# Reordering the two products of a mixture-of-experts half expert, and splitting softplus' eviction into deferred pieces

## The chip, the cores and the metric

One core of one Trainium2 chip runs the whole program. The metric is the device time of one execution in microseconds (us). The core's engines each work through a queue of their own, in order: TensorE (PE, matmuls and their weight loads PEld), VectorE (DVE), ScalarE (ACT), GpSimd (POOL) and SyncE (SP, which only issues DMAs here). TensorE accumulates in PSUM, in banks of 128 x 512 f32; the other operands are in SBUF.

## The reference

Three stages, all in float32: causal attention with a cumulative bias (2 batches, 8 heads, 576 tokens, head dimension 64), a mixture of 8 experts whose gates are balanced by 8 Sinkhorn steps, and a feed-forward layer with softplus. N = 1152 tokens, model width 512.

```python
def _moe_ref(x, w_gate, w1, w2):          # w1: 8 x 512 x 1024, w2: 8 x 1024 x 512
    ...                                   # P: gates, N x 8
    for e in range(E):
        h = np.maximum(x @ w1[e], 0.0)
        ye = h @ w2[e]
        out += P[:, e:e + 1] * ye

def _moe2_ref(x, w_in, w_out):            # 512 x 2048, 2048 x 512
    h = x @ w_in
    g = np.maximum(h, 0.0) + np.log1p(np.exp(-np.abs(h)))
    return (g @ w_out).astype(np.float32)
```

## The kernel before, in words

After attention, both feed-forward stages run as one loop over 20 half experts x of 512 hidden columns: 0 to 15 with Relu (two for each of 8 experts), 16 to 19 with softplus (the second layer). Every f32 operand is split into a high part in fp32r and a low part (xh and xl, w1h and w1l, w2h and w2l, hh and hl), and each product is three matmuls: high by high, high by low, low by high.

The first product, h = x @ w1, is done by Strassen's scheme. A Unit is one part p (of two) of a half expert's columns for one batch g of 576 tokens, and has seven products p1 to p7 of six matmuls with 288 columns each. Products accumulate in PSUM banks: the bank a takes p1, p6, p5, p3; the bank c takes p7 and p4; p2 has a bank of its own. Between products ScalarE copies a out to SBUF (v1 after p1, u2 after p6, u4 after p5), and since the next product adds to the same bank, TensorE waits for the copy. VectorE adds the copies to the other banks (t1 after p2, t2 after p5 and p4) and each result is evicted: for Relu hh = Relu(z) on ScalarE and hl = max(z, 0) - hh on VectorE. For softplus the eviction is Abs, Exp, Ln on ScalarE, two sums on VectorE, one on POOL, and then, in `post`, POOL's last sum, ScalarE's copy into hh and VectorE's difference hl.

The second product is written as rows: one of nine tiles of 128 tokens (`downs`), each of four quarters of three matmuls with 512 columns, after which the result is added into acc by VectorE (by ScalarE's copy in the first half of each layer). A row reads hh and hl of all four column blocks. Row 4 straddles the two batches. Rows use two PSUM banks in turn, so row t + 2 waits for the sum of row t.

The order on each engine is the order in which this Python code records instructions; no scheduler moves them. `late` holds evictions that are put off: each product ends with `flush()`, which records them all. `back` holds preparations (prep1 splits w1 of the next half, prep2 splits w2 of this one); `bg()` records one step of them. `quarter()` records a quarter of a row, a step of `bg` and, every so often, a step of the gates (in the first two halves) or of `convert`, which turns the second layer's float64 weights into f32 in pieces of 512 columns on VectorE, ScalarE and POOL and writes them to DRAM from POOL's queue. `turn` transposes acc for the second layer: batch 0 beside the last rows of half 15, batch 1 at the start of half 16.

Of a half's four Units, (p 0, batch 0) runs beside rows 5 to 8 of the half before. The next three run without rows beside them: (0, 1), (1, 0) and (1, 1) as far as p7, 18 products. The rest of the last one, p5, p3, p4, runs beside rows 0 to 3 (in halves 0 and 16 the first Unit runs without rows too, 25 products):

```python
for z in "dddPdddPdddPddddddd":            # d: a quarter, P: a product of the last Unit
...
for z in "PddPddPddPdPdddPddPdddd":        # P: a product of the next half's first Unit
```

## Time and profile before

| what | value |
|---|---|
| median of 3 runs (lowest, highest) | 1327.45 us (1326.55, 1327.57) |
| the profiled execution | 1327.69 us, span 1325.9 us |
| PE, PEld busy | 1127.5 us (85%), 975.9 us (74%) |
| DVE, ACT, POOL busy | 825.1 us (62%), 539.1 us (41%), 393.6 us (30%) |

Busy time is a share of the whole span, and the span has stages with different limits, so the stages are read apart. Attention ends near 122 us; the 16 ReLU half experts follow until 953 us, the four softplus half experts until 1321.5 us. In the profile's 40 slices of some 33 us TensorE is busy for nine tenths or more from slice 9 to slice 29, and for four to seven tenths, with one slice of nine, in the last ten; the granted clock is full in the former and 0.6 to 0.9 in the latter. An engine's idle time matters only where TensorE, or what ends the stage, waits for it.

### The profile page before, as it was taken

To read this page: it belongs to the slowest core of one execution; us is meant where nothing else is said; L and a number is where in the kernel's file an instruction comes from. 1 tells how busy PE (TensorE), PEld (TensorE's weight loads), DVE (VectorE), ACT (ScalarE), POOL (GpSimd) and SP (SyncE) were. 2 spreads that over 40 slices of the span, in tenths; PEclk is the share of its full clock that TensorE was granted. 3 is DMA by queue.
4 is the path that set the end of the run, shared out by engine and by line. 5 is a ranking of instruction groups with operands and counts; after the bars stand their busy time and mean duration, and the time that the engine had idled before them with its cause. 6 is when DMAs were issued, how large, how long until landed. Compare 5 with 4: busy or idle time off the path is not lost.

```text
span 1325.9 us, 17763 instructions
## 1 busy us (share of the span) xinstructions
PE 1127.5 (85%) x6596; PEld 975.9 (74%) x6596; DVE 825.1 (62%) x1575; ACT 539.1 (41%) x1138; POOL 393.6 (30%) x489
## 2 busy tenths in 40 slices
PE   6998998999999999999999999999954946756747
PEld 4766876888888888888888888889743745645635
DVE  4545456587877877877877876455554344545432
ACT  5977432234333333333233233233354444344431
POOL 8864000021312312322232222110124334334331
PEclk8978999999999999999999999999966978877869
DMA  5310101132312222222122221011010000000001
GB/s 161 106 42 13 48 33 44 35 110 73 118 58 96 100 75 96 83 86 96 71 96 96 80 74 62 32 65 48 17 32 0 33 32 17 20 29 16 0 2 71
DMA packets 30423, 78.47 MB, mean 59 GB/s; under 512 B 6048, under 2 KB 10656, under 8 KB 30336
## 3 DMA queue, kind: packets, MB, share of 16 engines
q1 hardware_dynamic: 27768, 68.93, 15.8%
q0 software_dynamic: 2560, 8.39, 1.7%
q8 instruction: 52, 0.85, 0.3%
q14 instruction: 35, 0.29, 0.1%
q10 hardware_dynamic: 8, 0.01, 0.0%
HBM read 66.02 MB, written 10.82 MB: 58 GB/s over the span
## 4 chain that ended last, share of the span: by engine, by line
PE 48%; DVE 22%; ACT 10%; POOL 10%; issue 8%; DMA 1%; SPq 0%; POOLq 0%; DVEq 0%; ACTq 0%
PE py L276 22%; PE ph L211 20%; POOL a L189 4%; DVE hl L171 3%; DVE acc L286 2%; DVE a L185 2%; PE sc L449 2%; POOL a L186 2%; ACT hh L190 2%; ACT a L181 1%; DVE t L233 1%; ACT hh L170 1%; ACT a L180 1%; DVE t L261 1%; PE pv L560 1%
## 5 line engine op out<-in xcount | busy, mean ns | idle before, releaser
L211 PE MATMUL ph<-xh,w1h 128*128 128x288 f32 x1120 | 351.9, 314 | 155.2 <-ACT u L219 124.2
L211 PEld LDWEIGHTS ph<-xh,w1h 128*128 128x128 f32 x1120 | 221.1, 197 | 184.0 <-ACT u L219 136.8
L211 PE MATMUL ph<-xl,w1h 128*128 128x288 f32 x1120 | 341.3, 305 | 0.0
L211 PE MATMUL ph<-xh,w1l 128*128 128x288 f32 x1120 | 340.8, 304 | 0.0
L276 PE MATMUL py<-w2h,hh 128*128 128x512 f32 x720 | 291.0, 404 | 16.0 <-DVE acc L283 13.1
L276 PE MATMUL py<-w2l,hh 128*128 128x512 f32 x720 | 289.1, 401 | 0.0
L276 PE MATMUL py<-w2h,hl 128*128 128x512 f32 x720 | 288.7, 401 | 0.0
L211 PEld LDWEIGHTS ph<-xl,w1h 128*128 128x128 f32 x1120 | 221.9, 198 | 8.2
L211 PEld LDWEIGHTS ph<-xh,w1l 128*128 128x128 f32 x1120 | 221.3, 198 | 0.0
L276 PEld LDWEIGHTS py<-w2h,hh 128*128 128x128 f32 x720 | 138.3, 192 | 41.5 <-DVE acc L283 14.5
L783 POOL TENSOR_TENSOR cm<-cm,ct 128x512 f32<-128x512 f32 x32 | 41.1, 1284 | 419.1 <-DVE ct L782 412.5
L276 PEld LDWEIGHTS py<-w2h,hl 128*128 128x128 f32 x720 | 138.2, 192 | 34.0
L276 PEld LDWEIGHTS py<-w2l,hh 128*128 128x128 f32 x720 | 138.2, 192 | 23.6
L170 ACT ACTIVATE hh<-t 128x288 fp32r<-128x288 f32 (+1 forms) x128 | 72.3, 565 | 189.3 <-DVE t L261 107.5
L171 DVE SCALAR_TENSOR_TENSOR hl<-t,hh 128x288 fp32r<-128x288 f32 (+1 forms) x128 | 84.2, 658 | 71.9 <-ACT hh L170 71.9
L186 POOL TENSOR_TENSOR a<-a,a 128x288 f32<-128x288 f32 x64 | 55.0, 860 | 210.2 <-DVE a L184 210.2
L219 ACT ACTIVATE u<-ph 128x288 f32<-128x288 f32 x160 | 64.6, 404 | 125.8 <-PE ph L211 125.8
L286 DVE SCALAR_TENSOR_TENSOR acc<-py,gate,acc 128x512 f32<-128x512 f32 x126 | 94.1, 747 | 29.0 <-PE py L276 28.0
L125 POOL TENSOR_TENSOR ws<-raw 128x256 f32<-128x256 f32 x40 | 31.7, 793 | 206.4 <-DVE w1l L136 148.3
L251 DVE TENSOR_TENSOR t<-ph,u 128x288 f32<-128x288 f32 x80 | 36.4, 455 | 78.8 <-ACT u L219 78.8
L191 DVE TENSOR_TENSOR hl<-a,hh 128x288 fp32r<-128x288 f32 x64 | 32.5, 508 | 84.8 <-ACT hh L190 84.8
L190 ACT ACTIVATE hh<-a 128x288 fp32r<-128x288 f32 x64 | 28.4, 443 | 95.3 <-POOL a L189 95.3
(176 smaller groups left out, 1590.1 us busy)
## 6 DMA issues: line engine op xcount, KB each, us to landing
...
```

The source lines that it names most:

```text
L170: nc.scalar.activation(out=hh, in_=src, func=AF.Relu)
L171: nc.vector.scalar_tensor_tensor(out=hl, in0=src, scalar=0.0, in1=f(hh), op0=ALU.max, op1=ALU.subtract)
L186: nc.gpsimd.tensor_tensor(out=a2, in0=a1, in1=a2, op=ALU.subtract)
L189: nc.gpsimd.tensor_tensor(out=a3, in0=a3, in1=a2, op=ALU.add)
L190: nc.scalar.activation(out=zh, in_=a3, func=AF.Copy)
L191: nc.vector.tensor_tensor(out=zl, in0=a3, in1=f(zh), op=ALU.subtract)
L211: nc.tensor.matmul(o, u, v, start=(start and c == 0 and n == 0), stop=(c == 1 and n == 2), skip_group_check=True)
L219: nc.scalar.activation(out=t, in_=self.a, func=AF.Copy)
L251: nc.vector.tensor_tensor(out=self.t2[:, HB:], in0=self.c, in1=u4, op=ALU.add)
L276: nc.tensor.matmul(py, u, v, start=(k == 0 and n == 0), stop=(k == NF - 1 and n == 2))
L286: nc.vector.scalar_tensor_tensor(out=a, in0=py, scalar=gate_t[0][:, t, e:e + 1], in1=a, op0=ALU.mult, op1=ALU.add)
L783: nc.gpsimd.tensor_tensor(out=m, in0=m, in1=f(t), op=ALU.add)
```

## The change

1. All four Units change places. `products(x, g)` makes a table of the 14 products of both parts, named a1 to a7 (part 0) and b1 to b7 (part 1), in the order a1 a2 a6 a7 a5 b1 b2 a3 a4 b6 b7 b5 b3 b4. Of batch 1, a1 a2 a6 a7 a5 run without rows; the other nine run beside rows 0 to 3. All 14 of the next half's batch 0 run beside rows 5 to 8. (Halves 0 and 16 first run 12 products of batch 0, then a1 a2 of batch 1 and b3 b4 of batch 0.) The counts of products and quarters are the same.
2. Deferred work carries a number of flushes to wait (`defer`), every quarter begins with a flush as well, and `drain` records all that is left. In the softplus halves a piece's VectorE and POOL sums (`sums`) come two flushes after its ScalarE operations, and the two last sums (`rest_`) five after (in the first stretch of half 16, one and two).
3. A softplus piece is 288 columns. POOL writes hh itself, ScalarE's copy goes, and VectorE makes hl in two sums, a3 - hh and then + a2.
4. p2's and p4's sums are written back into their PSUM banks, and evictions read them there; only p5's sum still goes to SBUF.
5. w2l is made in two sums of 512 columns for each half of w2, the second half's on POOL. A conversion item is recorded in four steps in place of two, at every third quarter in place of every sixth. Batch 1's transposes use the rows' banks.

```diff
         yield
-        nc.vector.tensor_tensor(out=lo, in0=t, in1=f(hi), op=ALU.subtract)
+        for c in range(2):
+            (nc.gpsimd if i else nc.vector).tensor_tensor(out=lo[:, c], in0=t[:, c], in1=f(hi[:, c]), op=ALU.subtract)
         load_next()
...
     late = []
+    def defer(k, x):
+        late.append([k, x])
     def flush():
-        for x in late:
+        now_ = [x for x in late if x[0] <= 0]
+        wait = [[k - 1, x] for k, x in late if k > 0]
+        late.clear()
+        for _, x in now_:
             x()
-        late.clear()
...
+        late[:0] = wait
+    def drain():
+        while late:
+            flush()
+    lag = [0, 1]
+    def evict(x, z, q, cols):
         hh, hl = hb[0][:, q, cols], hb[1][:, q, cols]
         if x < NX:
...
             return
...
+        def sums():
             nc.vector.tensor_scalar(a2, a1, 1.0, -1.0, ALU.add, ALU.add)
...
             nc.gpsimd.tensor_tensor(out=a2, in0=a1, in1=a2, op=ALU.subtract)
...
+            nc.gpsimd.tensor_tensor(out=hh, in0=a3, in1=a2, op=ALU.add)
+        def rest_():
+            nc.vector.tensor_tensor(out=a3, in0=a3, in1=f(hh), op=ALU.subtract)
+            nc.vector.tensor_tensor(out=hl, in0=a3, in1=a2, op=ALU.add)
+        defer(lag[0], sums)
+        defer(lag[1], rest_)
     class Unit:
...
             self.h1 = slice(g * S + HB, (g + 1) * S)
...
             flush()
-            t = m_t[0].tile([P, HB], F32, tag="t1", name="t1", bufs=1)
-            nc.vector.tensor_tensor(out=t, in0=b, in1=self.v1, op=ALU.add)
...
+            nc.vector.tensor_tensor(out=b, in0=b, in1=self.v1, op=ALU.add)
+            defer(0, lambda: evict(self.x, b, self.p, self.h0))
         def p6(self):
...
             u4 = self.copy("u4")
-            self.t2 = m_t[0].tile([P, S], F32, tag="t2", name="t2", bufs=1)
-            nc.vector.tensor_tensor(out=self.t2[:, HB:], in0=self.c, in1=u4, op=ALU.add)
+            t = m_t[0].tile([P, HB], F32, tag="t2", name="t2", bufs=2)
+            nc.vector.tensor_tensor(out=t, in0=self.c, in1=u4, op=ALU.add)
+            defer(0, lambda: evict(self.x, t, self.p + 2, self.h1))
         def p3(self):
...
             flush()
-            nc.vector.tensor_tensor(out=self.t2[:, :HB], in0=self.c, in1=self.u2, op=ALU.add)
...
+            nc.vector.tensor_tensor(out=self.c, in0=self.c, in1=self.u2, op=ALU.add)
+            defer(0, lambda: evict(self.x, self.c, self.p + 2, self.h0))
     def downs(x, tiles):
...
                 nc.vector.tensor_scalar(t, hi, 5, 2, ALU.logical_shift_left, ALU.logical_shift_right)
+                yield
                 nc.vector.scalar_tensor_tensor(out=t, in0=lo, scalar=29, in1=t,
...
                 nc.vector.tensor_scalar(t, t, 0xFF800000, None, ALU.bitwise_and)
+                yield
                 nc.vector.tensor_scalar(lo, lo, 28, 1, ALU.logical_shift_right, ALU.bitwise_and)
...
         def quarter(d):
+            flush()
             next(d, None)
...
             nstep[0] += 1
-            if x < 2:
-                if nstep[0] % 3 == 0:
+            if nstep[0] % 3 == 0:
+                if x < XE:
                     next(gates, None)
-            elif x < NX - 2 and nstep[0] % 6 == 0:
-                next(conv, None)
...
-        for x in range(NH):
...
+                elif x < NX - 2:
+                    next(conv, None)
+        ORDER = "a1 a2 a6 a7 a5 b1 b2 a3 a4 b6 b7 b5 b3 b4".split()
+        def products(x, g):
+            u = dict(a=Unit(x, 0, g), b=Unit(x, 1, g))
+            return {z: getattr(u[z[0]], "p" + z[1]) for z in ORDER}
+        def play(seq, todo, d=None):
+            for z in seq.split():
+                if z == "d":
+                    quarter(d)
+                else:
+                    todo.pop(z)()
+                    if d is None:
+                        bg()
         for x in range(NH):
...
             if x == NX:
...
             back += [prep2(x, 0), prep2(x, 1)]
+            c = {}
+            if first:
+                if x == NX:
+                    back.insert(0, turn(1, t_p))
+                c = products(x, 0)
+                for _ in range(2 if x == NX else 1):
+                    bg()
+                for z in ORDER[:-2]:
+                    c.pop(z)()
+                    bg(2 if x == NX else 1)
+                rest()
+            u = products(x, 1)
+            play("a1 a2", u)
+            if c:
+                play("b3 b4", c)
             if x == NX:
...
-                    rest()
...
+                drain()
...
+                lag[:] = [1, 4]
+            play("a6 a7 a5", u)
             rest()
...
+            drain()
+            d = downs(x, range(NB))
+            play("b1 d b2 d a3 d a4 d", u, d)
             back.append(prep1(x + 1, 0))
-            d = downs(x, range(NB))
...
-                    quarter(d)
+            play("b6 d b7 d b5 d d b3 d b4 d d d d d d d", u, d)
             rest()
+            drain()
             back.append(prep1(x + 1, 1))
             d = downs(x, range(NB, NTT))
-            for _ in range(NF):
-                quarter(d)
+            play("d d d d", {}, d)
             if x + 1 == NX:
...
                 for _ in range(4 * NF):
+                    flush()
                     next(d, None)
...
             elif x + 1 < NH:
...
-                        quarter(d)
+                u = products(x + 1, 0)
+                play("a1 d a2 d a6 d d a7 d a5 d", u, d)
+                rest()
+                play("b1 d b2 d a3 d a4 d b6 d b7 d b5 d d b3 d b4 d", u, d)
             for _ in d:
-                pass
+                flush()
             rest()
...
+        drain()
...
```
Three places in the queues, before and after. In the rows a number behind a name tells buffers apart.

VectorE in ReLU half 8, between the last row's sum and the sum after p2 (before) or a2 (after) of batch 1. L778 to L782 and L796, L797 belong to `convert`:

```order
L286 SCALAR_TENSOR_TENSOR acc<-py,gate,acc 128x512
L778 SCALAR_TENSOR_TENSOR cm<-cm,ct 128x512
L780 TENSOR_SCALAR ct<-ct 128x512
L781 TENSOR_SCALAR f_5476<-f_5476 128x512
L782 SCALAR_TENSOR_TENSOR ct<-f_5476,ct 128x512
L233 TENSOR_TENSOR t_5686<-ph,v_5674 128x288
L149 TENSOR_TENSOR w2l_5677<-raw,w2h_5676 128x1024
```

And after:

```order
L299 SCALAR_TENSOR_TENSOR acc<-py,gate,acc 128x512
L796 TENSOR_SCALAR f_5524<-f_5524 128x512
L797 SCALAR_TENSOR_TENSOR ct<-f_5524,ct 128x512
L245 TENSOR_TENSOR ph<-ph,v_5786 128x288
L150 TENSOR_TENSOR w2l_5789<-raw,w2h_5788 128x512 x2
L185 SCALAR_TENSOR_TENSOR hl<-ph,hh 128x288
```

Two of the four conversion operations have gone to an earlier quarter, p2's sum is written into its bank ph, and w2l is two operations, of the first half of w2 alone.

ScalarE in half 18, ahead of the copy u that p5 of the second part (b5) waits for. Before, the eviction of p4's t2 stands there:

```order
L180 ACTIVATE a_10612<-t_10549 128x288
L181 ACTIVATE a_10612<-a_10612 128x288
L182 ACTIVATE a_10614<-a_10612 128x288
L180 ACTIVATE a_10621<-t_10549 128x288
L181 ACTIVATE a_10621<-a_10621 128x288
L182 ACTIVATE a_10623<-a_10621 128x288
L190 ACTIVATE hh<-a_10614 128x288
L190 ACTIVATE hh<-a_10623 128x288
L219 ACTIVATE u_10636<-ph 128x288
```

After, the copy v of b1, and then the pieces b2, a3 and a4:

```order
L232 ACTIVATE v_10770<-ph 128x288
L191 ACTIVATE a_10784<-ph 128x288
L192 ACTIVATE a_10784<-a_10784 128x288
L193 ACTIVATE a_10786<-a_10784 128x288
L191 ACTIVATE a_10799<-ph 128x288
L192 ACTIVATE a_10799<-a_10799 128x288
L193 ACTIVATE a_10801<-a_10799 128x288
L191 ACTIVATE a_10823<-ph 128x288
L192 ACTIVATE a_10823<-a_10823 128x288
L193 ACTIVATE a_10825<-a_10823 128x288
L232 ACTIVATE u_10847<-ph 128x288
```

The two copies into hh (L190), which read POOL's sum, have gone; in front of u there are now three pieces of three operations where two pieces and their two copies were.

POOL in half 18 where w2 is split, before (the sums of four pieces; w2l is not POOL's):

```order
L186 TENSOR_TENSOR a_10469<-a_10468,a_10469 128x288
L189 TENSOR_TENSOR a_10461<-a_10461,a_10460 128x288
L189 TENSOR_TENSOR a_10470<-a_10470,a_10469 128x288
L186 TENSOR_TENSOR a_10515<-a_10514,a_10515 128x288
L189 TENSOR_TENSOR a_10516<-a_10516,a_10515 128x288
L186 TENSOR_TENSOR a_10576<-a_10575,a_10576 128x288
L189 TENSOR_TENSOR a_10577<-a_10577,a_10576 128x288
```

After (L150 is w2l of the second half of w2; a_10666 belongs to b4 of batch 0, a_10712 to a2 of batch 1, a_10750 to a5):

```order
L199 TENSOR_TENSOR a_10666<-a_10665,a_10666 128x288
L200 TENSOR_TENSOR hh<-a_10667,a_10666 128x288
L150 TENSOR_TENSOR w2l_10720<-raw,w2h_10719 128x512 x2
L199 TENSOR_TENSOR a_10712<-a_10711,a_10712 128x288
L200 TENSOR_TENSOR hh<-a_10713,a_10712 128x288
L199 TENSOR_TENSOR a_10750<-a_10749,a_10750 128x288
L200 TENSOR_TENSOR hh<-a_10751,a_10750 128x288
```

The two w2l operations stand between b4's sums and a2's, and VectorE's queue holds, at that place:

```order
L197 TENSOR_SCALAR a_10666<-a_10665 128x288
L198 SCALAR_TENSOR_TENSOR a_10667<-ph,a_10667 128x288
L245 TENSOR_TENSOR ph<-ph,v_10688 128x288
L150 TENSOR_TENSOR w2l_10691<-raw,w2h_10690 128x512 x2
L203 TENSOR_TENSOR a_10667<-a_10667,hh 128x288
L204 TENSOR_TENSOR hl<-a_10667,a_10666 128x288
L197 TENSOR_SCALAR a_10712<-a_10711 128x288
L198 SCALAR_TENSOR_TENSOR a_10713<-ph,a_10713 128x288
L263 TENSOR_TENSOR t_10747<-ph,u_10745 128x288
L203 TENSOR_TENSOR a_10713<-a_10713,hh 128x288
L204 TENSOR_TENSOR hl<-a_10713,a_10712 128x288
L197 TENSOR_SCALAR a_10750<-a_10749 128x288
```

There rest_ of a2 (L203, L204) stands ahead of the sums of a5, and ahead of it a2's sum L245 stands behind the sums of b4.

## Rows read from the trace of the kernel before

**Rows 1.** Stretches: us; PE, PEld, DVE, ACT, POOL busy (count); PEclk, DMA share, GB/s
```profile
302.40:812.40 510.00, 485.92 (x2761) 426.29 (x2760) 407.73 (x626) 175.64 (x329) 134.63 (x144) 1.00 0.26 86
812.40:908.30 95.90, 95.65 (x553) 85.37 (x552) 50.19 (x78) 31.52 (x60) 11.91 (x16) 1.00 0.14 45
953.30:1012.50 59.20, 29.64 (x172) 28.44 (x171) 32.56 (x57) 29.71 (x63) 16.87 (x21) 0.71 0.06 18
1061.60:1238.70 177.10, 113.66 (x553) 99.08 (x552) 82.08 (x149) 74.92 (x165) 67.63 (x80) 0.83 0.06 21
1238.70:1321.50 82.80, 51.12 (x235) 43.84 (x233) 32.66 (x63) 29.22 (x67) 23.04 (x28) 0.81 0.07 26
```

**Rows 2.** Timeline of TensorE, ReLU half 8 (start us, us, engine, line, operation)
```profile
607.70 0.40 PE L276 MATMUL py<-w2h,hh 128*128 128x512 f32 x1
...
608.40 0.30 PE L211 MATMUL ph<-xh,w1h 128*128 128x288 f32 x1
...
609.20 0.30 PE L211 MATMUL ph<-xh,w1h 128*128 128x288 f32 x1
```

**Rows 3.** Waits of TensorE, 302.4 to 812.4 (us in total, times, longest)
```profile
PE ph L211 <- ACT u L219: 13.3, 20, 0.9
PE ph L211 <- DVE t L251: 7.9, 10, 0.8
```

**Rows 4.** Timeline of VectorE, 608.3 to 612 us
```profile
608.60 0.75 DVE L286 SCALAR_TENSOR_TENSOR acc<-py,gate,acc 128x512 f32<-128x512 f32 x1 [0.83 <-PE py L276]
...
610.33 0.42 DVE L781 TENSOR_SCALAR f<-f 128x512 uint32<-128x512 uint32 x1
610.78 0.69 DVE L782 SCALAR_TENSOR_TENSOR ct<-f,ct 128x512 f32<-128x512 uint32 x1
611.39 0.45 DVE L233 TENSOR_TENSOR t<-ph,v 128x288 f32<-128x288 f32 x1
```

**Rows 5.** Waits of TensorE, the softplus stage
```profile
PE ph L211 <- ACT u L219: 107.5, 14, 13.9
```

**Rows 6.** Timeline of ScalarE, softplus half 18
```profile
1178.63 0.44 ACT L190 ACTIVATE hh<-a 128x288 fp32r<-128x288 f32 x1 [1.92 <-POOL a L189]
1179.38 0.44 ACT L190 ACTIVATE hh<-a 128x288 fp32r<-128x288 f32 x1 [0.31 <-POOL a L189]
1179.73 0.39 ACT L219 ACTIVATE u<-ph 128x288 f32<-128x288 f32 x1
```

**Rows 7.** Timeline of TensorE at the same place
```profile
1180.17 0.61 PE L211 MATMUL ph<-xh,w1h 128*128 128x288 f32 x1 [11.13 <-ACT u L219]
1180.58 0.45 PE L211 MATMUL ph<-xl,w1h 128*128 128x288 f32 x1
1180.82 0.45 PE L211 MATMUL ph<-xh,w1l 128*128 128x288 f32 x1
```

**Rows 8.** Forms in half 18 (1150 to 1238.7): count | busy us, mean ns | idle before
```profile
L185 DVE SCALAR_TENSOR_TENSOR a<-t,a 128x288 f32<-128x288 f32 x12 | 9.6, 797 | 1.4 <-ACT a L182 1.2
L191 DVE TENSOR_TENSOR hl<-a,hh 128x288 fp32r<-128x288 f32 x16 | 8.2, 514 | 21.3 <-ACT hh L190 21.3
L184 DVE TENSOR_SCALAR a<-a 128x288 f32<-128x288 f32 x16 | 4.9, 306 | 11.5 <-ACT a L181 11.5
L185 DVE SCALAR_TENSOR_TENSOR a<-ph,a 128x288 f32<-128x288 f32 x4 | 1.8, 458 | 0.7 <-ACT a L182 0.7
L186 POOL TENSOR_TENSOR a<-a,a 128x288 f32<-128x288 f32 x16 | 13.9, 867 | 52.9 <-DVE a L184 52.9
L189 POOL TENSOR_TENSOR a<-a,a 128x288 f32<-128x288 f32 x16 | 12.5, 792 | 1.8 <-DVE a L185 1.4
L182 ACT ACTIVATE a<-a 128x288 f32<-128x288 f32 x16 | 7.1, 444 | 0.5
```

**Rows 9.** Costliest groups of the page, the conversion's POOL sum
```profile
L783 POOL TENSOR_TENSOR cm<-cm,ct 128x512 f32<-128x512 f32 x32 | 41.1, 1284 | 419.1 <-DVE ct L782 412.5
```

More of the change, by code (lines that the diff above doesn't have):

```diff
@@ L159, in attention_moe_ffn @@
     late = []
+    def defer(k, x):
+        late.append([k, x])
     def flush():
-        for x in late:
-            x()
-        late.clear()
-    def evict(x, src, q, cols):
+        now_ = [x for x in late if x[0] <= 0]
+        wait = [[k - 1, x] for k, x in late if k > 0]
+        late.clear()
+        for _, x in now_:
+            x()
+        late[:0] = wait
[4 more added lines that the diff above has]
+    def evict(x, z, q, cols):
         hh, hl = hb[0][:, q, cols], hb[1][:, q, cols]
         if x < NX:
-            nc.scalar.activation(out=hh, in_=src, func=AF.Relu)
-            nc.vector.scalar_tensor_tensor(out=hl, in0=src, scalar=0.0, in1=f(hh), op0=ALU.max, op1=ALU.subtract)
+            nc.scalar.activation(out=hh, in_=z, func=AF.Relu)
+            nc.vector.scalar_tensor_tensor(out=hl, in0=z, scalar=0.0, in1=f(hh), op0=ALU.max, op1=ALU.subtract)
             return
-        m3 = m3_t[0]
-        n = cols.stop - cols.start
-        for a in range(0, n, HB):
-            z, zh, zl = src[:, a:a + HB], hh[:, a:a + HB], hl[:, a:a + HB]
-            a1 = m3.tile([P, HB], F32, tag="a1", name="a1")
-            a2 = m3.tile([P, HB], F32, tag="a2", name="a2")
-            a3 = m3.tile([P, HB], F32, tag="a3", name="a3")
-            nc.scalar.activation(out=a1, in_=z, func=AF.Abs)
-            nc.scalar.activation(out=a1, in_=a1, func=AF.Exp, scale=-1.0)
-            nc.scalar.activation(out=a3, in_=a1, func=AF.Ln, bias=1.0)
+        m3 = m3_t[-1]
+        a1 = m3.tile([P, HB], F32, tag="a1", name="a1")
+        a2 = m3.tile([P, HB], F32, tag="a2", name="a2")
+        a3 = m3.tile([P, HB], F32, tag="a3", name="a3")
+        nc.scalar.activation(out=a1, in_=z, func=AF.Abs)
+        nc.scalar.activation(out=a1, in_=a1, func=AF.Exp, scale=-1.0)
+        nc.scalar.activation(out=a3, in_=a1, func=AF.Ln, bias=1.0)
+        def sums():
             nc.vector.tensor_scalar(a2, a1, 1.0, -1.0, ALU.add, ALU.add)
@@ L186, in evict @@
             nc.gpsimd.tensor_tensor(out=a2, in0=a1, in1=a2, op=ALU.subtract)
-            def post(a2=a2, a3=a3, zh=zh, zl=zl):
-                nc.gpsimd.tensor_tensor(out=a3, in0=a3, in1=a2, op=ALU.add)
-                nc.scalar.activation(out=zh, in_=a3, func=AF.Copy)
-                nc.vector.tensor_tensor(out=zl, in0=a3, in1=f(zh), op=ALU.subtract)
-            late.append(post)
+            nc.gpsimd.tensor_tensor(out=hh, in0=a3, in1=a2, op=ALU.add)
[4 more added lines that the diff above has]
+        defer(lag[1], rest_)
     class Unit:
@@ L201, in __init__ @@
             self.h1 = slice(g * S + HB, (g + 1) * S)
-            self.both = slice(g * S, (g + 1) * S)
         def product(self, o, a, b, start):
@@ L798, in turn @@
             for c in (0, 2, 1, 3):
-                px = ps.tile([P, 512], F32, tag="tr", name="px", bufs=2)
+                px = bank(1 + c // 2)
                 for t in range(NB):
@@ L855, in attention_moe_ffn @@
-            k = 2 if x == NX else 1
-            prev = None
-            for u in parts[x][0 if first else 1:]:
-                last = u is parts[x][-1]
-                if x == NX and u is parts[x][2]:
-                    rest()
-                u.p1()
-                bg(k)
-                u.p2()
-                bg(k)
-                if prev:
-                    prev.p3()
-                    prev.p4()
-                    bg(k)
-                u.p6()
-                bg(k)
-                u.p7()
-                if not last:
-                    bg(k)
-                    u.p5()
-                    bg(k)
-                prev = u
+            c = {}
```

31 lines of the change are left out of this document (8 added, 23 removed).

## The prediction

> **What bounds the kernel now.** I read the table of stretches first. In the ten middle ReLU half experts (302.4 to 812.4 us) one takes 51.0 us, in two later ones (812.4 to 908.3) 47.95, both at the full clock; the four softplus half experts, 953.3 to 1321.5 us, take 368.2 us at clocks of 0.71 to 0.83 [rows 1]. Then TensorE's timeline: a quarter of a row (three matmuls of 512) takes 608.40 - 607.70 = 0.70 us, a Strassen product (six of 288) 609.20 - 608.40 = 0.80 [rows 2]. A half expert has 28 products and 36 quarters: 22.4 + 25.2 = 47.6 us if TensorE never waits. So the later ReLU halves run at TensorE's own pace, the ten middle ones lose 3.4 us each, and the softplus stage, 4 x 47.6 = 190.4 at that pace, loses 177.8.
>
> Third, TensorE's waits. In the ten middle halves it waits twice a half for the ScalarE copy u (13.3 us in all) and once for VectorE's t (7.9): 2.1 us each half, the rest mostly the restarts behind them [rows 3]. They lie where products run without rows beside them. The first is late because four conversion pieces stand between row 8's sum, begun at 608.60, and the sum t that ScalarE's next instruction needs, begun at 611.39 [rows 4]. In the softplus stage 107.5 of the lost us are one wait, 14 times: products behind the copy u, up to 13.9 us [rows 5]. ScalarE's timeline shows why: u, at 1179.73, stands behind two copies hh, the first of which waits 1.92 us for POOL's sums [rows 6]. TensorE then starts at half clock, 0.24 us from one matmul of 288 to the next (1180.58 to 1180.82) in place of 0.133 [rows 7].
>
> **The change, part by part.**
>
> *ReLU halves.* Five products of batch 1 stay without rows, where 18 stood; the other 23 have rows between them, so a copy or sum has some 1.5 us a step to be made in, not 0.8. The waits for t and for the second u go: quarters now stand in front of both readers. The first u stays (a5 reads the bank that it copies), but two conversion pieces stand ahead of its sum in place of four: 0.42 + 0.69 us [rows 4]. From row 8's end: its sum to 1.0, pieces 2.0, a2's sum 2.45, Relu 2.95, u 3.35; a5 is wanted at 3.2, so 0.2 late, plus a restart of up to 0.3. With 0.4 for small losses beside the rows, 0.9 us of 3.4 are left: 2.5 x 10 = 25 us gained. The later ReLU halves have nothing to give. For the first three, whose gate and first conversion steps come at the same count of quarters but with products between, I take 5 us. Together 30. Bounds: 13 (VectorE, busy 407.7 of 510 us [rows 1], holds one product up by 0.8 to 1.0 twice a half) and 42 (3.4 x 10, and 8).
>
> Half of w2l goes to POOL: two sums of 512, each 1.28 us by the conversion's sum of that size [rows 9]. ScalarE's second w2h ends at 4.4, so they are ready at 5.7 and 7.0; row 0's second quarter reads the first at 3.5 + 0.8 + 0.8 + 0.7 + 0.8 + 0.2 = 6.8. Hidden, with 1.1 us to spare. The next load of raw is issued behind them, some 3 us later, over 10 us before its reader. The joint eviction of 576 becomes two of 288: some 0.1 us on two engines, under products.
>
> *Softplus pieces.* There are 16 pieces of 288 a half. Each loses ScalarE's copy hh (0.44) and gains a second VectorE sum in place of hl; POOL's two sums stay. The forms: Ln 0.44 (Abs and Exp alike); TENSOR_SCALAR 0.31; max-and-add 0.80 with z in SBUF, 0.46 with z in PSUM; hl 0.51; POOL 0.87 and 0.79 [rows 8]. Three of four pieces now have z in PSUM, before one of four. VectorE is busy 82.1 / 2 = 41 us a half [rows 1], 24.5 of them pieces; new pieces are 16 x (0.31 + 0.55 + 1.02) = 30, so 41 - 24.5 + 30 - 1.2 (w2l) = 45. POOL 33.8 + 2.6 = 36.4, ScalarE 37.5 - 7.1 = 30.4. None exceeds TensorE's 47.6, so the order in the queues decides. I lay a steady half out by hand, each engine in its program order, T = 0 where a1 of batch 1 starts, with these durations (VectorE's second of two sums 0.37 after the first, a pair beside POOL 0.85):
>
> - ScalarE copies v1 only behind b4 of batch 0, whose Abs waits for a sum in PSUM: 4.2. a6, wanted at 1.6, loses 2.6.
> - a2's sum stands on VectorE behind rest(b5), row 8's sum, rest(b3) and sums(b4): 5.5. Behind it three ScalarE operations (1.42) and u2: 7.4. a5, wanted at 5.9, loses 1.5 and ends at 8.35.
> - POOL takes the two w2l sums at 8.5, when ScalarE has made w2h, and a2's pair only then: 8.5 + 2.6 + 1.7 = 12.7. rest(a2) waits for it with all of VectorE behind it, idle some 3 us: 13.5; sums(a5) 14.3; POOL again; rest(a5) 16.4; b2's sum 16.8, of a product that ended at 10. ScalarE does b2 to 18.2 and a3 to 19.7, VectorE sums(a3) 20.35 and a4's sum 20.75, ScalarE a4 to 22.2 and u2 of b6 22.6. b5 is wanted at 8.35 + 6 x 0.80 + 6 x 0.70 = 17.35: 5.3 lost.
> - b4 waits for b5's sum, 1.1; row 4 for row 2's sum, which stands behind rest(b3) and sums(b4), 3.4.
> - Beside rows 5 to 8, the same two kinds of wait: b5 0.8, b4 1.2.
>
> In sum 15.9, and 1.5 for matmuls at half clock (the rest of that lies where VectorE is behind anyway): 47.6 + 17.4 = 65 us. Half 16's first 19 products, without rows and with batch 1's transposes, laid out alike, take 36 us, where 25 took 59.2 [rows 1]; there a4 and both w2h stand before a copy. The stage: 36, then 31.5 to row 4 and 25 to row 8; 65 x 2; 40 for the last half's products and rows 0 to 4, 12 for its last 16 quarters: 274.5. Gain 368.2 - 274.5 = 94. Bounds: 149 (rival 1) and 46 (rival 2).
>
> The Trainium skill ("SBUF — State Buffer", section "SBUF: two separate sides") says that a VectorE operation with two SBUF inputs and a GpSimd operation that reads SBUF shut each other out for a whole instruction. The trace agrees in direction: with POOL's sum beside both, the max-and-add takes 0.80 from SBUF, 0.46 from PSUM [rows 8]. By that rule the sums moved to PSUM gain, and the new rest sums and POOL's w2l lose; rival 2 is what the losing side would make.
>
> **Sum.** The profiled execution took 1327.69 us, 1.8 of it outside its span of 1325.9; that stays. The runs' median is 1327.45, 0.2 below. 1327.7 - 30 - 94 = 1203.7: 1204 us.
>
> **Rivals.**
> 1. *TensorE's own pace.* The lags (sums two steps late, rest five) empty the queues of waits, and a softplus half takes 51, one restart a stretch: 33 + 45 + 51 x 2 + 39 = 219, a gain of 149: 1149 us. For it: no engine has over 45 us of work. Against it: a2's sums behind w2l on POOL, and two drains a half that make VectorE wait for POOL.
> 2. *VectorE and POOL in each other's way.* Each of the 32 rest sums of a half has two SBUF inputs. If each pays what the max-and-add pays beside POOL, 0.80 - 0.46 = 0.34 us, that is 11 to 12 us a half on an engine through which the path runs: 77 a half, 48 over the stage: 1252. For it: POOL is busy 36 of 65 us. Against it: hl, with the same kind of inputs, has a mean of 0.51 today [rows 8].
> 3. *No gain in the ReLU halves.* VectorE's 41 us in 48 leave no slack beside 23 products, and its lateness comes back in b4 and a4: 51 us stay, 1204 + 25 = 1229. Against it: the three or more steps between each sum and its reader.
> 4. *Slower.* No row shows POOL writing fp32r, and hh and half of w2l now are written so by POOL. If that were four times slower (5.1 us a w2l sum), row 0 would wait for POOL in every half, some 5 us x 20, and a piece would hold POOL 4 us, 64 a half: 1204 + 100 + 12 x 4 = 1352. It begins at 2.4 us a w2l sum, where the 1.1 to spare are gone, and decides from near 4.8. Against it: ScalarE's hh in fp32r and Ln in f32 take 0.44 alike [rows 6, 8].
>
> **How the numbers follow.** Forecast 0.60 (5 us either way in a softplus half and the ReLU bounds give it 1180 to 1228), rivals 0.12, 0.17, 0.08 and 0.03. The range of 1168 to 1245 holds the forecast, rival 3 and the near parts of rivals 1 and 2. About 0.2%, 2.7 us, is what a measurement can tell from no change: faster 0.96, within it 0.01, slower 0.03.
>
> **What would show it.** Right: a middle ReLU half near 48.5 us with one wait for u left; a softplus half of 60 to 70; VectorE idle some 3 us for POOL ahead of rest(a2), with w2l before a2's sums on POOL; TensorE's longest wait of a half at b5 of batch 1, behind u. Wrong: rest sums of 0.8 us or more (rival 2), POOL sums that write fp32r well over those of today (rival 4), ReLU halves still at 51 (rival 3), softplus halves near 51 (rival 1).

## The result, and the profile after

The changed kernel takes 1243.73 us (median of 4 runs, 1241.68 to 1247.77); the kernel before took 1327.12 on the same chip. The ratio is 0.9376, 95% interval 0.9351 to 0.94. The forecast was 1204 in a range of 1168 to 1245: the softplus halves gained nearly what was forecast, the ReLU halves nothing, and the whole is 40 us short, at the upper end of the range. The profiled execution has a span of 1242.9 us:

| stage, us | before | after | forecast |
|---|---|---|---|
| attention | 122.0 | 118.0 | no change |
| 16 ReLU halves | 831.3 | 837.9 | 30 less |
| four softplus halves | 368.2 | 282.6 | 274.5 |
| after the last half | 4.4 | 4.4 | no change |

Attention's code is as it was; over the experiments below it ended anywhere from 116.2 to 123.3 us. So the softplus halves gave the gain, 85.6 us, and the ReLU halves, forecast to give 30 us, took 6.6 longer. The miss is thus 36.6 us in the ReLU halves and 8.1 in the softplus halves; 4.0 of it are hidden by an attention that happened to be shorter, which is luck.

The table of stretches answers to [rows 1]. First the ten middle ReLU halves, then the two later ones, then softplus halves 17 and 18 together:

```profile
307.20:819.80 512.60, 485.46 (x2761) 429.43 (x2760) 405.25 (x664) 182.98 (x369) 159.25 (x160) 0.99 0.25 86
819.80:914.90 95.10, 95.10 (x553) 85.16 (x552) 49.91 (x86) 33.30 (x68) 16.90 (x20) 1.00 0.13 45
...
1049.95:1186.35 136.40, 109.41 (x554) 92.79 (x553) 96.92 (x182) 60.24 (x134) 73.36 (x85) 0.91 0.08 28
```

A middle half takes 51.3 us (51.0 before); a later one 47.55, with TensorE never idle. A steady softplus half takes 68.2.

What the middle halves wait for, TensorE's waits from 307.2 to 819.8 us (us in all, times, longest), in place of [rows 3]:

```profile
PE ph L224 <- ACT v L232: 22.9, 10, 2.3
PE ph L224 <- ACT u L232: 4.2, 10, 0.4
```

The waits for t and the second u are gone, and the u left costs 0.4 us; but every half now waits once, 2.3 us, for v, for which it waited 0.3 before. It is a6 of the next half's batch 0, beside row 5, behind the copy v of a1. The timelines of POOL, ScalarE and TensorE around one such place show what v stands behind:

```profile
587.42 1.41 POOL L798 TENSOR_TENSOR cm<-cm,ct 128x512 f32<-128x512 f32 x1 [12.33 <-DVE ct L797]
...
589.70 0.75 POOL L125 TENSOR_TENSOR ws<-raw 128x256 f32<-128x256 f32 x1
...
592.98 1.18 POOL L130 TENSOR_TENSOR ws<-raw,ws 128x256 f32<-128x256 f32 x1
...
594.18 1.06 ACT L134 ACTIVATE w1h<-ws 128x1024 fp32r<-128x1024 f32 x1 [5.07 <-POOL ws L130]
595.15 0.39 ACT L232 ACTIVATE v<-ph 128x288 f32<-128x288 f32 x1
...
595.59 0.40 PE L224 MATMUL ph<-xh,w1h 128*128 128x288 f32 x1 [2.29 <-ACT v L232]
```

ScalarE's second copy of w1h (L134, Strassen's sums of the next half's weights) is recorded one step ahead of v and waits 5.07 us for POOL, whose four sums of ws come behind the conversion's sum. In the new order a6, which reads the bank that v copies, follows a1 by a quarter, a2 and another quarter, some 2.2 us. In the later halves, without conversion, the same copies cost nothing.

In the softplus stage, TensorE's waits (answering to [rows 5], 107.5 us there):

```profile
PE ph L224 <- ACT u L232: 35.2, 10, 11.4
PE py L289 <- DVE acc L296: 9.4, 3, 3.4
PE ph L224 <- DVE t L263: 7.5, 7, 1.6
PE ph L224 <- ACT v L232: 7.2, 4, 2.5
```

Half 18's queues on POOL, then VectorE, where the forecast put its idle stretch ahead of rest(a2) (in place of [rows 6]):

```profile
1126.86 2.58 POOL L150 TENSOR_TENSOR w2l<-raw,w2h 128x512 fp32r<-128x512 f32 x2 [1.44 <-ACT w2h L147]
...
1130.28 0.80 POOL L200 TENSOR_TENSOR hh<-a,a 128x288 fp32r<-128x288 f32 x1
...
1127.43 0.46 DVE L263 TENSOR_TENSOR t<-ph,u 128x288 f32<-128x288 f32 x1
1131.12 0.46 DVE L203 TENSOR_TENSOR a<-a,hh 128x288 f32<-128x288 f32 x1 [3.22 <-POOL hh L200]
```

VectorE stands 3.22 us, with w2l ahead of a2's sums on POOL, as laid out; a w2l sum takes 1.29 us, as the conversion's of that size [rows 9]. What the pieces cost, the forms of half 18 (busy us, mean ns, idle before), in place of [rows 8]:

```profile
L203 DVE TENSOR_TENSOR a<-a,hh 128x288 f32<-128x288 f32 x16 | 9.8, 612 | 10.2 <-POOL hh L200 10.2
L204 DVE TENSOR_TENSOR hl<-a,a 128x288 fp32r<-128x288 f32 x16 | 9.6, 600 | 0.6
...
L198 DVE SCALAR_TENSOR_TENSOR a<-ph,a 128x288 f32<-128x288 f32 x12 | 5.4, 452 | 0.5 <-ACT a L193 0.5
...
L198 DVE SCALAR_TENSOR_TENSOR a<-t,a 128x288 f32<-128x288 f32 x5 | 4.6, 921 | 0.7 <-ACT a L193 0.7
...
L200 POOL TENSOR_TENSOR hh<-a,a 128x288 fp32r<-128x288 f32 x16 | 13.6, 848 | 2.5 <-DVE a L198 0.9 <-PE ph L224 0.5
```

In this half VectorE idles 10.2 us for POOL's hh ahead of rest sums: that is the largest idle of the engine, and the last experiments are about it.

### The profile page after: what moved, and what is told of

It is laid out like the page before. It is cut to its first block, busy times and chain, and to the rows that moved or that the text cites. A ratio compares the mean times of both kernels' runs of the same rounds, so it can differ in the third digit from the quotient of the medians.

```text
span 1242.9 us, 17931 instructions
## 1 busy us (share of the span) xinstructions
PE 1113.2 (90%) x6596; PEld 963.3 (78%) x6596; DVE 850.4 (68%) x1703; ACT 520.4 (42%) x1138; POOL 450.4 (36%) x529
## 4 chain that ended last, share of the span: by engine, by line
PE 42%; DVE 28%; POOL 10%; ACT 9%; issue 9%; DMA 1%; SPq 1%; DVEq 0%; POOLq 0%; ACTq 0%
PE py L289 19%; PE ph L224 17%; DVE hl L185 3%; ACT hh L184 3%; DVE a L203 2%; DVE hl L204 2%; DVE acc L299 2%; DVE w2l L150 2%; POOL hh L200 2%; PE sc L462 2%; DVE ph L274 1%; DVE w1l L136 1%; DVE a L198 1%; POOL a L199 1%; POOL cm L798 1%
## 5 line engine op out<-in xcount | busy, mean ns | idle before, releaser
L224 PE MATMUL ph<-xh,w1h 128*128 128x288 f32 x1120 | 344.3, 307 | 89.5 <-ACT u L232 44.5
L224 PE MATMUL ph<-xl,w1h 128*128 128x288 f32 x1120 | 336.7, 301 | 0.0
L224 PEld LDWEIGHTS ph<-xh,w1h 128*128 128x128 f32 x1120 | 216.2, 193 | 126.1 <-ACT u L232 52.5
L224 PEld LDWEIGHTS ph<-xl,w1h 128*128 128x128 f32 x1120 | 217.2, 194 | 18.7
L184 ACT ACTIVATE hh<-ph 128x288 fp32r<-128x288 f32 x192 | 78.3, 409 | 218.6 <-DVE ph L274 112.2
L289 PEld LDWEIGHTS py<-w2h,hh 128*128 128x128 f32 x720 | 140.2, 195 | 28.1 <-POOL a L199 10.6
L185 DVE SCALAR_TENSOR_TENSOR hl<-ph,hh 128x288 fp32r<-128x288 f32 x192 | 86.8, 455 | 62.0 <-ACT hh L184 60.2
L299 DVE SCALAR_TENSOR_TENSOR acc<-py,gate,acc 128x512 f32<-128x512 f32 x126 | 93.6, 743 | 36.5 <-PE py L289 36.5
L150 POOL TENSOR_TENSOR w2l<-raw,w2h 128x512 fp32r<-128x512 f32 x40 | 53.1, 1347 | 165.6 <-ACT w2h L147 165.4
L134 ACT ACTIVATE w1h<-ws 128x1024 fp32r<-128x1024 f32 x40 | 42.1, 1051 | 73.1 <-POOL ws L130 73.1
L185 DVE SCALAR_TENSOR_TENSOR hl<-t,hh 128x288 fp32r<-128x288 f32 x64 | 43.3, 677 | 32.7 <-ACT hh L184 32.7
L203 DVE TENSOR_TENSOR a<-a,hh 128x288 f32<-128x288 f32 x64 | 38.4, 601 | 39.7 <-POOL hh L200 39.7
```

The costliest lines, as they stand in the source:

```text
L134: nc.scalar.activation(out=hi[:, S1:], in_=s4, func=AF.Copy)
L150: (nc.gpsimd if i else nc.vector).tensor_tensor(out=lo[:, c], in0=t[:, c], in1=f(hi[:, c]), op=ALU.subtract)
L184: nc.scalar.activation(out=hh, in_=z, func=AF.Relu)
L185: nc.vector.scalar_tensor_tensor(out=hl, in0=z, scalar=0.0, in1=f(hh), op0=ALU.max, op1=ALU.subtract)
L203: nc.vector.tensor_tensor(out=a3, in0=a3, in1=f(hh), op=ALU.subtract)
L224: nc.tensor.matmul(o, u, v, start=(start and c == 0 and n == 0), stop=(c == 1 and n == 2), skip_group_check=True)
```

## The experiments

Ratios are to the kernel before, timed on the same chip, with the 95% interval.

### 1. w1h's second copy a quarter later

```diff
         yield
         yield
+        if x and p:
+            yield
         nc.scalar.activation(out=hi[:, S1:], in_=s4, func=AF.Copy)
```

> The changed kernel, with one edit: the second copy into w1h of part 1 (which waits for POOL's four sums into ws) is recorded one quarter later, so that it comes behind a1's copy v on ScalarE. Theory A (order of ScalarE's queue): beside row 5 TensorE waits 2.3 us at a6 in each of ten ReLU halves because v stands behind that copy; POOL stays as slow as it is, and the wait goes all the same. TensorE's waits for v from half 3 to 12 fall from 22.9 us to under 3, a middle half takes 48.2 to 48.6 us, the whole 25 to 30 us less than the changed kernel: 1214 to 1219 us. Theory B (POOL is too late for every reader): the same copy then stands before a2's Relu and u, and before w1l that b1 reads, so the wait comes back at a5 or b1: less than 8 us gained, 1236 us or more.

1211.65 us (1209.14 to 1213.86), ratio 0.9131 (0.9109 to 0.9154): 32 us less than the changed kernel, by theory A's mechanism and 2 us beyond its range. Its stretch of the ten middle halves, and TensorE's only wait in it:

```profile
305.15:787.29 482.14, 477.81 (x2762) 425.91 (x2760) 405.19 (x664) 182.27 (x370) 159.50 (x160) 1.00 0.27 91
```
```profile
PE ph L226 <- ACT u L234: 4.3, 10, 0.4
```

The wait for v is gone and nothing took its place; a middle half takes 48.2 us. The whole ReLU stage takes 802.0 us, 29.3 less than before. The queue of ScalarE is what kept the ReLU gain back.

In halves 3, 6 and 10 of the changed kernel the wait for v cost 4.0 us, in the other seven 2.5. The wait itself is 2.3 us in all ten; in those three the matmuls behind it run at half pace, as in half 10:

```profile
697.20 0.61 PE L224 MATMUL ph<-xh,w1h 128*128 128x288 f32 x1 [2.29 <-ACT v L232]
697.61 0.44 PE L224 MATMUL ph<-xl,w1h 128*128 128x288 f32 x1
697.85 0.44 PE L224 MATMUL ph<-xh,w1l 128*128 128x288 f32 x1
```

One follows the other by 0.24 us, where behind the wait shown for half 8 it is 0.13.

### 2. The softplus halves' w2l on VectorE

```diff
-            (nc.gpsimd if i else nc.vector).tensor_tensor(out=lo[:, c], ...)
+            (nc.gpsimd if i and x < NX else nc.vector).tensor_tensor(out=lo[:, c], ...)
```

> The changed kernel, with w2l of the second half of w2 back on VectorE in the softplus halves only (ReLU halves as changed). Theory A (POOL's queue): VectorE's 3.2 us of idle time ahead of a2's last sums goes, b5 of batch 1 waits 1 to 2 us in place of 3 to 4, a softplus half takes 65 to 66 us in place of 68, the whole 8 to 11 us less: 1233 to 1236. Theory B (VectorE's work is the bound of the stage): 1.24 us more of it a half, no gain or up to 5 us lost: 1244 to 1249.

1240.82 us (1240.12 to 1242.42), ratio 0.9347 (0.9329 to 0.9366). TensorE's wait for u over the stage:

```profile
PE ph L224 <- ACT u L232: 35.2, 10, 9.4
```

The same 35.2 us in all; the stage is 3.6 us shorter, which is no more than it varies between profiles of the same softplus code (279.6 in experiment 1, 284.0 in experiment 11). In half 18 VectorE still waits 8.7 us for POOL ahead of rest sums (10.2 in the changed kernel), 1.6 at most (3.22 there): the one long wait is gone, and others are in its place. TensorE waits 4.1 us at b5 there, 3.5 in the changed kernel. The time lies between the two theories' ranges, and neither is borne out.

### 3 and 4. One half of the change at a time

Experiment 3 keeps the old order and takes the new pieces (`evict`, `defer`, p2, p4 and p5 of the changed kernel, three buffers); experiment 4 keeps the new order and takes the old pieces:

```diff
-        def sums():
-            nc.vector.tensor_scalar(a2, a1, 1.0, -1.0, ALU.add, ALU.add)
...
+        nc.vector.tensor_scalar(a2, a1, 1.0, -1.0, ALU.add, ALU.add)
...
+        def post():
+            nc.gpsimd.tensor_tensor(out=a3, in0=a3, in1=a2, op=ALU.add)
+            nc.scalar.activation(out=hh, in_=a3, func=AF.Copy)
+            nc.vector.tensor_tensor(out=hl, in0=a3, in1=f(hh), op=ALU.subtract)
+        defer(0, post)
```

> One part alone: the old order of Units, products and rows, with the new softplus pieces (POOL writes hh, VectorE's two last sums, both deferred by flushes, evictions from PSUM; three buffers for the pieces). Theory A (what frees ScalarE's queue of copies that wait for POOL makes the gain): the softplus stage takes 300 to 325 us where 368 stood and 283 stand now, the ReLU halves 51.0 as before: 1262 to 1287. Theory B (rows between the products make the gain): 345 to 368 us for the stage, 1305 or more.

> The other part alone: the new order, flushes and conversion steps, with softplus' old operations (two sums on VectorE at once, POOL, then POOL's last sum, ScalarE's copy into hh and VectorE's hl at the next flush). Theory A (the copies hh in front of u make the waits, whatever stands between products): the softplus stage takes 325 to 360 us, TensorE's waits for u stay above 70 us, 1286 to 1320. Theory B (rows between the products hide them): 285 to 305 us, 1246 to 1266.

The pieces alone: 1241.91 us (1238.79 to 1245.04), ratio 0.9354 (0.9316 to 0.9392). The order alone: 1317.07 (1313.62 to 1320.79), ratio 0.9923 (0.9894 to 0.9952). The softplus stage of the first and its longest kind of wait:

```profile
959.50:1238.80 279.30, 223.97 (x1124) 194.52 (x1124) 200.02 (x367) 128.34 (x281) 134.71 (x154) 0.88 0.09 29
```
```profile
PE ph L223 <- ACT u L231: 39.3, 13, 10.0
```

And of the second:

```profile
954.07:1308.50 354.43, 228.65 (x1119) 196.83 (x1117) 153.51 (x300) 154.64 (x344) 137.88 (x162) 0.80 0.07 23
```
```profile
PE ph L221 <- ACT u L229: 84.7, 13, 13.1
```

The pieces alone give the whole gain, 20 us more of it than theory A had; the order alone came as theory A had it. What stood in u's way before is a wait of ScalarE in the softplus stage:

```profile
ACT hh L190 <- POOL a L189: 95.3, 64, 2.1
```

With the new order and the old pieces this wait is 107.2 us. With the new pieces ScalarE makes no such copy, and TensorE's waits for u fall from 107.5 us to 39.3. The sums p2 and p4 left in PSUM don't make this gain, since experiment 4 has them too. Whether it is the copy that has gone or the sums that are put off was not tried apart.

The order gains 14 us of softplus stage on the old pieces and nothing that shows on the new ones (282.6 against 279.3). Its worth lies in the ReLU halves, together with the split conversion, and experiment 1 brings it out: with the pieces alone a middle half takes 51.4 us.

### 5. A third buffer in half 16

```diff
-                m3_t.append(tp.enter_context(tc.tile_pool(name="m3", bufs=2, ...)))
+                m3_t.append(tp.enter_context(tc.tile_pool(name="m3", bufs=3, ...)))
```

> The changed kernel with the first experiment's edit (w1h's second copy a quarter later; 1211.65 us by itself) and a third buffer for the pieces' tiles a1, a2, a3 in the first part of half 16, where there are two. There batch 0's b5 waits 10.9 us for ScalarE's u, and ScalarE's Ln ahead of u waits 3.68 us for VectorE's hl, the last reader of the tile that Ln writes. Theory A: the two buffers make the wait; b5 falls to 4 or 5 us and the whole to 1204 to 1207 us. Rival B: VectorE is late anyway (two w2l sums of 1.2 and 1.3 us and rest sums of 1.4 us stand ahead), so that the Relu-free queue of ScalarE meets the same lateness at the next tile: b5 still over 9 us, 1210 to 1213 us.

1210.89 us (1208.81 to 1215.06), ratio 0.9132 (0.9101 to 0.9163): no change. ScalarE's longest wait around b5, in experiment 1 and then here:

```profile
ACT a L195 <- DVE hl L206: 3.7, 1, 3.7
```
```profile
ACT a L193 <- DVE t L265: 6.9, 2, 4.8
```

The wait for the buffer went, as theory A had it, and ScalarE waits for VectorE one instruction on; the wait at b5 falls from 10.0 to 7.8 us, and half 16 still takes 94.1 us. By time it is rival B: VectorE was late, and the buffer only the first place where it showed.

### 6 and 9. acc's sum ahead of the pieces

A softplus half's fifth row waits 3.6 us for row 2's sum. Experiment 6 moves the flush at a row's end, in `downs`, behind that sum; experiment 9 has the flush of a quarter behind the quarter (both on experiment 1):

```diff
-            flush()
+            if x < NX:
+                flush()
...
                                               op0=ALU.mult, op1=ALU.add)
+            if x >= NX:
+                flush()
```

Experiment 9 leaves the last two lines of that out, and in `quarter`:

```diff
-            flush()
+            if x < NX:
+                flush()
             next(d, None)
+            if x >= NX:
+                flush()
```

> The first experiment's kernel (1211.65 us), with one thing swapped in the softplus halves: at the end of a row its sum into acc is recorded ahead of the put-off sums of the pieces, not behind them. Row 4 waits 3.6 us in halves 17 and 18 and 2.5 in half 16 for row 2's sum, which stands behind rest(b3) and sums(b4). Theory A: the wait falls to 1 us or less and stays away, since the pieces delayed by one sum of some 0.7 us have steps to spare: 7 to 9 us off the whole, 1203 to 1205 us. Rival B: the lateness is VectorE's and only changes place, to the waits for u (36.0 us in all) and t (5.7): 1209 to 1212 us.

> The first experiment's kernel (1211.65 us); in the softplus halves the put-off pieces are recorded behind each quarter, not ahead of it, so that acc's sum, which a quarter records when it ends a row, stands ahead of them on VectorE (in the sixth experiment they still stood ahead, as the queue shows: row 4's wait stayed at 3.8 us behind rest(b3) and sums(b4)). Theory A: row 4's wait of 3.6 us in halves 17 and 18 falls to 1 us or less and is not given back: 5 to 8 us off, 1203 to 1207 us. Rival B: VectorE's lateness comes from waiting for POOL's hh (10.2 us in half 18) and is given back at b5, b4 or a5: 1208 to 1212 us.

Experiment 6: 1206.89 us (1206.4 to 1209.26), ratio 0.9101 (0.907 to 0.9133), between the two theories' ranges. It missed its aim, as VectorE's timeline ahead of row 4 shows:

```profile
1120.75 0.46 DVE L205 TENSOR_TENSOR a<-a,hh 128x288 f32<-128x288 f32 x1 [1.05 <-POOL hh L202]
...
1121.62 0.30 DVE L199 TENSOR_SCALAR a<-a 128x288 f32<-128x288 f32 x1
1121.84 0.45 DVE L200 SCALAR_TENSOR_TENSOR a<-ph,a 128x288 f32<-128x288 f32 x1
1122.21 0.68 DVE L299 TENSOR_TENSOR acc<-py,acc 128x512 f32<-128x512 f32 x1
```

The sum (L299) still stands behind a rest and a pair of sums, since the quarter's own flush records them first. Experiment 9: 1199.62 us (1196.73 to 1201.47), ratio 0.904 (0.9013 to 0.9067), 12 us less than experiment 1 and below both ranges. Its waits for acc and t over the stage:

```profile
PE ph L226 <- DVE t L265: 4.3, 6, 1.8
PE py L291 <- DVE hl L206: 3.8, 4, 1.2
PE py L291 <- DVE acc L299: 2.8, 2, 1.4
```

acc's waits fall from 8.2 to 2.8 us and t's from 5.7 to 4.3, hl's rise to 3.8 and u's from 36.0 to 39.2: in waits nearly all is given back, as rival B had it. Yet the stage is 8.1 us shorter (271.5), theory A's size. The difference lies in TensorE's busy time, 220.1 us in experiment 1 and 213.6 here, at granted clocks of 0.88 and 0.91: fewer matmuls run at half pace. Part of that varies by itself: experiment 5, whose code differs from experiment 1's in half 16 alone, has 216.4 us at 0.92. The edit does a second thing, too: with the flush at a row's end left out, each row has one flush fewer, so the put-off sums come later, and VectorE's wait for POOL's hh falls from 39.0 to 33.3 us over the stage. The two aren't told apart.

### 7. p2's and p4's sums in SBUF

```diff
-            nc.vector.tensor_tensor(out=b, in0=b, in1=self.v1, op=ALU.add)
-            defer(0, lambda: evict(self.x, b, self.p, self.h0))
+            t = m_t[0].tile([P, HB], F32, tag="t1", name="t1", bufs=1)
+            nc.vector.tensor_tensor(out=t, in0=b, in1=self.v1, op=ALU.add)
+            defer(0, lambda: evict(self.x, t, self.p, self.h0))
```

p4 is edited alike, with a tile t4.

> The first experiment's kernel (1211.65 us) with the sums of p2 and p4 written to SBUF tiles, as the kernel before did, in place of PSUM; the rest of the change stays. Eight of a half's sixteen pieces then read z from SBUF: the max-and-add 0.8 to 1.04 us in place of 0.46, 2.7 to 4.6 us of VectorE in a softplus half. Theory A: VectorE stands on the path in the softplus halves, so most of it shows: 10 to 16 us in four halves, 1221 to 1228 us. Rival B: it lies beside waits for POOL and ScalarE: 1211 to 1216 us. The middle ReLU halves stay at 48.2 us by both.

1222.08 us (1218.65 to 1223.67), ratio 0.9209 (0.9179 to 0.9238): 10 us more than experiment 1. The max-and-add with z in SBUF, half 18:

```profile
L200 DVE SCALAR_TENSOR_TENSOR a<-t,a 128x288 f32<-128x288 f32 x13 | 10.5, 809 | 0.9 <-ACT a L195 0.8
```

Some 7 us of it lie in the softplus stage (286.9 against 279.6), and 3 in the middle ReLU halves (48.53 against 48.21), which both theories had left alone. The total is theory A's; VectorE is on the softplus path.

### 8. Experiments 1, 2, 5 and 6 together

> The first experiment's edit, w2l of the softplus halves on VectorE alone (the second experiment's edit), the third buffer of half 16 and acc's sum first, together. If each removes its own wait (3.6 us for w2l as measured, 6 for the buffer, 7 for acc): 1194 to 1198 us. If they only shift one lateness of VectorE from wait to wait, the sum of the parts isn't reached: 1203 to 1210 us.

1201.88 us (1199.92 to 1205.71), ratio 0.9063 (0.9033 to 0.9094). That lies between the two, nearer the second. The forecast sum isn't reached, since neither the buffer nor the moved flush gave what it was meant to; what the three edits gave by themselves (2.9, 0.8 and 4.8 us) does come together, 9.8 us.

### 10. A longer lag for the rest sums

```diff
-                m3_t.append(ctx.enter_context(tc.tile_pool(name="m3b", bufs=4, ...)))
-                lag[:] = [1, 4]
+                m3_t.append(ctx.enter_context(tc.tile_pool(name="m3b", bufs=6, ...)))
+                lag[:] = [1, 7]
```

> The first experiment's kernel (1211.65 us) with the rest sums put off by eight pieces of the program in place of five, and six buffers for the pieces' tiles in place of four. VectorE waits 10.2 us in half 18 for POOL's hh ahead of a rest sum, with the sums that ScalarE and TensorE want behind it. Theory A: these waits set the softplus half; they fall to 3 us or less, and TensorE's waits for u with them: 3 to 5 us a half, 1196 to 1204 us. Rival B: the path runs through the chain of one piece (sum, three ScalarE operations, two VectorE, two POOL), and the drains make the rest sums come together anyway: 1209 to 1213 us.

1193.98 us (1192.19 to 1195.19), ratio 0.8999 (0.898 to 0.9019), the fastest kernel here. VectorE's wait for POOL over the softplus stage, in experiment 1 and then here:

```profile
DVE a L205 <- POOL hh L202: 39.0, 30, 3.2
```
```profile
DVE a L205 <- POOL hh L202: 5.1, 5, 1.4
```

TensorE's waits over the stage, and the stage itself:

```profile
PE ph L226 <- ACT u L234: 35.8, 13, 11.4
...
PE py L291 <- DVE acc L298: 3.3, 2, 1.9
PE ph L226 <- DVE t L265: 2.4, 2, 1.2
```
```profile
920.25:1186.00 265.75, 215.68 (x1119) 186.96 (x1117) 207.55 (x364) 127.85 (x281) 145.38 (x162) 0.90 0.09 30
```

Theory A by size, 13.9 us of stage and 2 us beyond its range, but not in the waits that it named: those for u stay (36.0 before), those for acc and t fall from 13.9 us to 5.7, v's from 7.2 to 6.0, and TensorE's busy time from 220.1 us to 215.7 (granted clock 0.88 and 0.90).

### 11. The conversion undivided

```diff
                 nc.vector.tensor_scalar(t, hi, 5, 2, ...)
-                yield
                 nc.vector.scalar_tensor_tensor(out=t, in0=lo, scalar=29, in1=t, ...)
```

The second new yield goes too, and `next(conv)` comes at every sixth quarter.

> The first experiment's kernel (1211.65 us) with the conversion in two pieces, one every sixth quarter, as in the kernel before, in place of four, one every third; the rest of the change stays. The split was there so that two, not four, VectorE instructions stand ahead of a sum. Theory A: some sum that a product waits for now meets all four: a5's wait grows from 0.6 to 1.5 to 2.5 us in the middle halves, 10 to 20 us in all, 1221 to 1231 us. Rival B: with rows between the products the four pieces are hidden where they fall: 1208 to 1215 us.

1227.98 us (1223.78 to 1233.24), ratio 0.9259 (0.9226 to 0.9291): 16 us more. TensorE's wait for u in the ten middle halves, 4.3 us in experiment 1:

```profile
PE ph L226 <- ACT u L234: 14.9, 10, 1.5
```

A middle half takes 49.46 us against 48.21: 12.5 us over ten, 10.6 of them this wait at a5. Theory A; the split carries its share of the change. The rest of the 16 us is mostly the softplus stage, 284.0 us for 279.6 with the same code.

### 12. Experiments 1, 2, 9 and 10 together

> Together: w1h's second copy a quarter later (1211.65 us by itself), the longer lag with six buffers (with it 1193.98), the pieces recorded behind a quarter (with the first 1199.62) and w2l of the softplus halves on VectorE (3 us off the changed kernel). Theory A: acc's sum still waits 3.3 us in all with the longer lag, and w2l still stands ahead of a2's sums on POOL, so each gives a little more: 1186 to 1191 us. Rival B: all three only freed VectorE from waiting for POOL, which the lag alone does (0.7 us left in half 18): 1192 to 1196 us.

1195.08 us (1191.57 to 1197.67, 5 runs), ratio 0.9008 (0.8984 to 0.9032): no better than experiment 10. A wait of its own appears in the stage:

```profile
PE py L291 <- DVE hl L206: 9.1, 4, 3.3
```

Row 4 waits for hl. With the longer lag more rest sums are left for the `drain` ahead of row 4, and those of a row's end now stand behind acc's sum: that is my reading, not tried by itself. Rival B by size.

## Why the prediction was right and where it was short

*What bounds the kernel, and the softplus pieces: right.* The gain is the pieces' (experiments 3 and 4), and the step named, hh out of ScalarE's queue, fits: its 95.3 us of waits for POOL are gone. The sums put off came with it and aren't told apart from it. POOL writes fp32r at the price of f32 (0.85 us a sum, 0.81 for the f32 one), so rival 4 is wrong. POOL and ScalarE are busy 36.7 and 29.9 us in half 18 (36.4 and 30.4 forecast), VectorE 48.7 (45): the two rest sums cost 0.61 and 0.60 us, not 1.02 together, which is 3.0 of the 3.7 us.

*VectorE beside POOL.* Of the 41 of each kind of rest sum from 1015 to 1190 us two in three take 0.46 us, the slowest 1.05 and 0.95; the max-and-add takes 0.45 from PSUM and 0.92 on the mean from SBUF. POOL's own sums are slowed at most from 0.80 to 1.12. The Trainium skill ("SBUF — State Buffer", section "SBUF: two separate sides") has each fully block the other for a whole instruction. The direction agrees: the 13 of each kind that fall beside a POOL sum take 0.81 to 1.05 us. The other 28 fall beside none. Rival 2 had each pay 0.34 us over the forecast's 0.51; 0.10 is what came on the mean, because two in three meet no sum of POOL, not because a meeting is cheap.

*The layout of a steady half: waits right in sum, restarts too small.* For half 18 forecast and found: a6 2.6 and 2.2, a5 1.5 and 2.7, b5 5.3 and 3.6, b4 1.1 and 1.8, row 4 3.4 and 3.6, beside rows 5 to 8 2.0 and 1.6; 15.9 and 15.5 in sum. The sum is closer than its parts, which is luck: b5 is 1.7 us too long, a5 and b4 together 1.9 too short. Nor does b5's wait hang on w2l as laid out, since it stays without w2l on POOL (experiment 2). The term that failed is "1.5 for matmuls at half clock". TensorE's timeline behind b5, which answers to [rows 7]:

```profile
1140.94 0.61 PE L224 MATMUL ph<-xh,w1h 128*128 128x288 f32 x1 [3.48 <-ACT u L232]
...
1141.58 0.44 PE L224 MATMUL ph<-xh,w1l 128*128 128x288 f32 x1
1141.82 0.44 PE L224 MATMUL ph<-xh,w1h 128*128 128x288 f32 x1
...
1142.97 0.63 PE L289 MATMUL py<-w2l,hh 128*128 128x512 f32 x1
1143.40 0.63 PE L289 MATMUL py<-w2h,hl 128*128 128x512 f32 x1
...
1145.13 0.29 PE L224 MATMUL ph<-xh,w1h 128*128 128x288 f32 x1
1145.26 0.29 PE L224 MATMUL ph<-xl,w1h 128*128 128x288 f32 x1
```

After the wait one matmul of 288 follows another by 0.24 us, one of 512 by 0.43, and only at 1144.5 is the spacing back at 0.13. A product loses 0.8 us so, a quarter 0.6, and 68.5 - 47.6 - 15.5 = 5.4 us a half, not 1.5. Some 1.6 us each lie behind a5, b5 and row 4. The forecast took most of that to lie where VectorE is late anyway; it shows in full. The two steady halves, 136.4 us for 130, are 6.4 of the 8.1 by which the stage is longer than 274.5; half 16 (94.0 for 92.5) is most of the rest, and hides errors that cancel: its first 19 products take 39.8 us for 36, the rest 54.2 for 56.5.

*The ReLU halves: the step that failed.* The forecast kept 0.9 us of 3.4, "with 0.4 for small losses beside the rows". Without rows a half loses 0.7 us now (2.9 before), beside rows 0 to 4 nothing, as forecast; beside rows 5 to 8 it loses 2.5 to 4.0 at a6. That stretch I had not laid out for the ReLU halves: there ScalarE's copy of w1h waits for POOL behind the conversion's sum, ahead of v. Take that away (experiment 1) and a middle half takes 48.2 us (48.5 forecast) and the stage gains 29.3 (30): 27.9 in the ten middle halves (25), 1.4 in the other six (5). So the outcome was rival 3's 51 us, but not its mechanism: b4 and a4 never wait in these halves, and VectorE, with 405 us of work in the 482 of experiment 1, has slack enough.

*The parts.* What of the change is worth what, on the kernel of experiment 1: the split of the conversion 16 us (12.5 of them in the middle halves), the sums in PSUM 10. w2l on POOL makes TensorE wait nowhere in the middle ReLU halves; in the softplus halves its cost can't be told from no change.

*Open:* what sets b5's wait of a steady half, which is 3.2 to 4.6 us in half 18 of experiments 1, 2 and 10, with and without VectorE's waits for POOL; half 16's wait at b5, 9 to 12 us long, 7.8 with a third buffer, which gained nothing; and why the old order, with other waits, does as well in the softplus stage as the new one.
